# Giving out the last FFN step of each group behind the next group's first score product

## Chip, cores, metric

One core of one Trainium2 chip. The metric is the device time of one execution in microseconds (us), median of several; lower is better. The kernels of an experiment are timed in rounds together with the kernel before, on the same chip. Profiles are taken once per kernel; the profiled span leaves out some 2 us of the time at the ends, so spans are compared with spans and times with times.

## The reference, cut to what matters

```python
# attention: B,H,S,D = 4,8,768,48; a complex gate per element, normalised to a magnitude <= 0.999
for t in range(S):
    S_re, S_im = ar*S_re - ai*S_im + kv, ar*S_im + ai*S_re     # kv = k_t outer v_t
    y[:, :, t] = einsum('bhd,bhde->bhe', q[:, :, t], S_re)
x = y.transpose(0, 2, 1, 3).reshape(3072, 384)
# maxout FFN: d_ff = 768
h = maximum(maximum(x @ w1, x @ w2), x @ w3)
out = h @ w_out
```

## The kernel before

The kernel works in tiles of 128 tokens, two tiles to a group (C = 2), twelve groups. For each tile TensorE makes two score products **A** and **B**, a state product **dk**, transposes **tp** for the next tile, a small product **F**, suffix sums **sfx** and the attention output **y**. Between these the program weaves, as steps in a list, the gates of the next group (activations on ScalarE, products on VectorE and GpSimd, the small matmuls **mds** and **cs**) and the FFN of the group before: nine **up** steps (12 matmuls each for a whole group) and two **out** steps (**op**, 12 matmuls each, one for each tile).

```python
def weave(*streams):                       # steps of each stream spread evenly over its range
    order = []
    for si, (begin, end, steps) in enumerate(streams):
        n = len(steps)
        for i, step in enumerate(steps):
            order.append((begin + (end - begin) * (i + 0.5) / n, si, i, step))
    for _, _, _, step in sorted(order, key=lambda e: e[:3]):
        step()
...
def outputs(x, xs):                        # the y product, then its copy to SBUF, on ScalarE
    ...
    nc.scalar.copy(out=T["xT", xs[-1]][:, :, o:o + P], in_=y)                    # L575
...
def up_step(xs, fp, i):
    ps = psM.tile(...)                                                           # psM: 4 PSUM buffers
    for j in range(2):
        for d in range(KD):
            nc.tensor.matmul(out=ps[:, j], lhsT=ws[i][...], rhs=xT[:, d], ...)   # L589: needs xT
    if i == 0: nc.scalar.copy(out=dst, in_=ps)
    else:      nc.vector.tensor_tensor(out=dst, in0=dst, in1=ps, op=OP.max)      # L594: hT
def out_step(xs, x):
    for f in range(KF):
        nc.tensor.matmul(out=ps, lhsT=hT[:, f, o:o + P], rhs=wo[:, f], ...)      # L600: doesn't need xT
    nc.scalar.copy(out=ot, in_=ps); nc.sync.dma_start(out=out[...], in_=ot)
...
def tile_steps(x):
    return [scores A, gather A, scores B] + tp[:1] + [gather B, state] + tp[1:] + F + ... + [outputs] + ...
...
for g in range(1, NG):
    ...
    ffn = ffn_steps(tokens(g * C - 1))     # nine up, two out (group 1: the FFN of one tile, 9 + 1)
    def feed(n):                           # also called twice from within the gates, before cs
        for _ in range(min(n, len(ffn))):
            ffn.pop(0)()
    weave((0.0, 1.0, tile_steps(g * C) + tile_steps(g * C + 1)), (0.0, 0.7, pre_steps(g + 1, feed)),
          (0.0, 1.0 if g > 1 else 0.5, [call(feed, 1) for _ in ffn]))
for f in ffn_steps(tokens(NX - 1)):        # the tail: the FFN of the last group
    f()
```

The lines of the helpers are the same in the changed kernel, as the change stands below them. Where an experiment adds lines above, its profile shows them two or three higher.

## Time and profile before

| | before |
|---|---|
| time, median of 3 | 742.48 us (742.40 to 744.02) |
| profiled span, mean granted TensorE clock | 740.5 us, 0.970 |
| TensorE busy | 670.2 us, 91% |
| wait of up for xT | 6.6 us in 9 waits |

TensorE is the engine that sets the time; the waits, the steady group and the first groups are shown and read in the prediction below. Two more lines of the page: the shares by engine of the chain of work that ended last, and the costliest group of instructions, whose last field is TensorE's idle time in front of it and what ended most of that.

```profile
PE 71%; issue 13%; DVE 7%; ACT 6%; DMA 1%; POOL 1%; SPq 0%; ACTq 0%; POOLq 0%; DVEq 0%
...
L589 PE MATMUL up<-xT,w 128*128 128x256 f32 (+1 forms) x1404 | 297.5, 365 | 6.7 <-ACT xT L575 6.6
```

ScalarE, 54% busy, still has 6% of the chain: its queue in front of the xT copy.

### The profile page before, as it was taken

Reading aid. Unit: us, or ns where it says so; the run is one execution under the profiler, and the core shown is the slowest. Engines: PE = TensorE matmul, PEld = TensorE weight load, DVE = VectorE, ACT = ScalarE, POOL = GpSimd, SP = SyncE. Lnnn points to the kernel's source line nnn. Section 1 sums busy time; section 2 is a strip of 40 time slices with the busy share of each in tenths; the row PEclk is TensorE's granted clock in tenths of the full one; section 3 lists DMA queues with packets and bytes.
Section 4 is the critical chain, followed back from the end, with each engine's and each line's share of the span. In section 5 each row is a group of like instructions: output and inputs, shape, how many; then the busy total and the mean of one; then the engine's idle time right before and its main releaser. Section 6 shows DMA issues by size and latency. Waiting matters only on the chain.

```text
span 740.5 us, 17637 instructions
## 1 busy us (share of the span) xinstructions
PE 670.2 (91%) x7620; PEld 540.8 (73%) x7620; DVE 521.2 (70%) x718; ACT 400.8 (54%) x677; POOL 117.1 (16%) x121
## 2 busy tenths in 40 slices
PE   1266779789999999999999999999999999999998
PEld 0055668578778878878878778778778778778785
DVE  5999998897857867767757767767767677565210
ACT  6778655567556566466466466466475465322000
POOL 9200000403104004004005005004004004000000
PEclk9687799999999999999999999999999999999999
DMA  9780432140410410410410410410410210000000
GB/s 220 212 187 12 107 108 45 30 91 12 85 35 10 89 34 9 91 34 12 86 34 12 86 34 12 86 34 13 86 34 13 44 34 2 1 23 2 12 12 22
DMA packets 134158, 38.91 MB, mean 53 GB/s; under 512 B 126784, under 2 KB 129856, under 8 KB 134080
## 3 DMA queue, kind: packets, MB, share of 16 engines
q1 hardware_dynamic: 133824, 37.76, 23.0%
q8 instruction: 60, 0.98, 0.6%
q14 instruction: 18, 0.15, 0.1%
q10 hardware_dynamic: 256, 0.01, 0.0%
HBM read 33.03 MB, written 4.72 MB: 51 GB/s over the span
## 4 chain that ended last, share of the span: by engine, by line
PE 71%; issue 13%; DVE 7%; ACT 6%; DMA 1%; POOL 1%; SPq 0%; ACTq 0%; POOLq 0%; DVEq 0%
PE up L589 34%; PE op L600 12%; PE tp L442 5%; PE dk L539 4%; PE B L502 4%; PE y L567 3%; PE A L502 3%; ACT e L106 2%; PE mds L405 2%; PE cs L360 2%; PE sfx L405 2%; PE F L455 2%; ACT L L106 1%; ACT w L106 1%; PE cs L362 1%
## 5 line engine op out<-in xcount | busy, mean ns | idle before, releaser
L589 PE MATMUL up<-xT,w 128*128 128x256 f32 (+1 forms) x1404 | 297.5, 365 | 6.7 <-ACT xT L575 6.6
L589 PEld LDWEIGHTS up<-xT,w 128*128 128x128 f32 x1404 | 247.5, 190 | 46.2 <-ACT xT L575 8.9
L600 PE MATMUL op<-wo,hT 128*128 128x384 f32 x288 | 98.9, 492 | 7.3 <-DVE wo L292 3.9
L338 POOL TENSOR_TENSOR ai<-ai,L 128x768 f32<-128x768 f32 x10 | 25.8, 2578 | 382.4 <-ACT L L106 309.0
L600 PEld LDWEIGHTS op<-wo,hT 128*128 128x128 f32 x288 | 52.9, 191 | 41.5 <-issue 4.3
L594 DVE TENSOR_TENSOR hT<-hT,up 128x512 f32<-128x512 f32 (+1 forms) x78 | 49.8, 640 | 40.2 <-PE up L589 40.1
L469 DVE TENSOR_TENSOR Q<-Q,f 112x512 f32<-112x512 f32 x48 | 41.2, 857 | 42.0 <-ACT f L106 42.0
L444 ACT COPY K<-tp 112x512 f32<-112x512 f32 x48 | 27.9, 582 | 61.1 <-PE tp L442 61.0
L592 ACT COPY hT<-up 128x512 f32<-128x512 f32 (+1 forms) x39 | 21.4, 548 | 69.4 <-PE up L589 69.4
L602 ACT COPY ot<-op 128x384 f32<-128x384 f32 x24 | 11.5, 479 | 86.5 <-PE op L600 86.5
L551 DVE TENSOR_TENSOR g<-g,dk 112x384 f32<-112x384 f32 x40 | 22.1, 552 | 47.9 <-PE dk L539 47.4
L567 PEld LDWEIGHTS y<-atm,vb 128*32 128x32 f32 x1536 | 39.3, 111 | 13.9 <-issue 7.9
L539 PEld LDWEIGHTS dk<-vb,uk 128*112 128x112 f32 x384 | 42.0, 180 | 6.8 <-issue 2.5
L567 PE MATMUL y<-atm,vb 128*32 128x64 f32 x1536 | 46.6, 223 | 0.4 <-DVE atm L520 0.4
L567 PE MATMUL y<-QG,g 112*32 112x64 f32 x1536 | 46.0, 221 | 0.0
L469 DVE TENSOR_TENSOR QB<-Q,f 112x512 f32<-112x512 f32 (+1 forms) x48 | 45.4, 982 | 0.0
L539 PE MATMUL dk<-vb,uk 128*112 128x96 f32 x384 | 42.4, 264 | 3.1 <-issue 2.3
L502 PE MATMUL B<-QB,KB 112*64 112x96 f32 x768 | 37.8, 252 | 7.3 <-DVE QB L469 7.3
L502 PEld LDWEIGHTS B<-QB,KB 112*64 112x64 f32 x768 | 33.8, 140 | 11.5 <-issue 10.9
L405 PE MATMUL mds<-Ln,mid 128*128 128x384 f32 x48 | 23.9, 582 | 20.1 <-POOL cuts L120 15.9
L106 ACT ACTIVATE f<-F 48x296 f32<-48x296 f32 x96 | 39.6, 413 | 1.4 <-PE F L455 0.2
L502 PE MATMUL A<-Q,K 112*64 112x96 f32 x768 | 37.7, 249 | 2.6 <-DVE Q L469 2.4
(111 smaller groups left out, 1111.9 us busy)
## 6 DMA issues: line engine op xcount, KB each, us to landing
ar<-in_a_re_dram SPq DMA_DIRECT2D x24, 192.0 KB, 3.7
ai<-in_a_im_dram SPq DMA_DIRECT2D x24, 192.0 KB, 3.9
k<-in_k_dram SPq DMA_DIRECT2D x24, 192.0 KB, 2.9
q<-in_q_dram SPq DMA_DIRECT2D x24, 192.0 KB, 3.0
vb<-in_v_dram SPq DMA_DIRECT2D x96, 48.0 KB, 2.4
out_dram<-ot SPq DMA_DIRECT2D x24, 192.0 KB, 1.9
raw<-in_moe_w_dram SPq DMA_DIRECT2D x5, 768.0 KB, 6.5
raw<-in_moe_w_out_dram SPq DMA_DIRECT2D x3, 768.0 KB, 4.4
```

The costliest lines, as they stand in the source:

```text
L106: tab(nc.scalar.activation(**kw))
L338: (nc.gpsimd if g > 1 else nc.vector).tensor_tensor(out=ai, in0=ai, in1=L, op=OP.mult)
L405: nc.tensor.matmul(out=ps, lhsT=mat, rhs=T["Ln", g][:, c * DM:(c + 1) * DM], start=True, stop=True)
L442: nc.tensor.transpose(out=tp[0:DD, j], in_=both(T["U" + nm, x], hg * HU + j), identity=ident)
L444: nc.scalar.copy(out=T["K", x][0:DD, hs], in_=tp[0:DD])
L469: nc.vector.tensor_tensor(out=out, in0=in_, in1=f.to_broadcast([DD, H, 2 * n, 8]), op=OP.mult)
L502: nc.tensor.matmul(out=ps[o:o + L64, h // HU, h % HU * 96:h % HU * 96 + 96], lhsT=K[0:DD, h, o:o + L64], rhs=Q[0:DD, 2 * h + c], start=Tru ...
L539: nc.tensor.matmul(out=ps[0:DD, h // HU, h % HU * 96:h % HU * 96 + 96], lhsT=both(T["Uk", x], h), rhs=T["v", x][:, :, h // 2, o:o + D], st ...
L567: nc.tensor.matmul(out=y[32 * (r % 4):32 * (r % 4) + 32, r // 4, c * L64:(c + 1) * L64], lhsT=V[:, c, i, lo:lo + 32] if new else G[0:DD, c ...
L589: nc.tensor.matmul(out=ps[:, j], lhsT=ws[i][:, d, f * P:(f + 1) * P], rhs=xT[:, d], start=(d == 0), stop=(d == KD - 1))
L594: nc.vector.tensor_tensor(out=dst, in0=dst, in1=ps, op=OP.max)
L600: nc.tensor.matmul(out=ps, lhsT=hT[:, f, o:o + P], rhs=wo[:, f], start=(f == 0), stop=(f == KF - 1))
```

## The change

The intent: when the first up step of a group comes up on TensorE, its input xT is not there yet. So the last step of the old list, an out step that needs no xT, is held back and given out first in the next group.

```diff
+    held = []
     for g in range(1, NG):
         load(g + 1, load_v)
         load(g + 2, load_a, load_kq)
-        ffn = ffn_steps(tokens(g * C - 1))
+        ffn = held + ffn_steps(tokens(g * C - 1))
+        held = [ffn.pop()]
         ...
-    for f in ffn_steps(tokens(NX - 1)):
+    for f in held + ffn_steps(tokens(NX - 1)):
         f()
```

## The prediction

> **What bounds the kernel now.** I read the head of the page first, then the list of TensorE's waits, then the timeline of one steady group (C = 2 tiles), engine by engine, and last the two ends of the run, where things differ.

> ```profile
> PE 670.2 (91%) x7620; PEld 540.8 (73%) x7620; DVE 521.2 (70%) x718; ACT 400.8 (54%) x677; POOL 117.1 (16%) x121
> PEclk9687799999999999999999999999999999999999
> ...
> PE cs L360 <- DVE w L356: 13.7, 3, 12.2
> PE up L589 <- ACT xT L575: 6.6, 9, 0.8
> PE op L600 <- DVE hT L594: 3.4, 1, 3.4
> ```

> The three last lines are of TensorE's waits: total, times, longest, in us. TensorE is busy 91% at a full granted clock after the start, and most of its idle time is in the first 160 us; the one wait that comes back is that of the FFN's first up product for xT, nine times. So from the third group on the kernel is as long as its TensorE stream plus 0.8 us per group. The timeline shows what is behind the 0.8 us, TensorE first and ScalarE after it:

> ```profile
> 436.20 1.54 PE L502 MATMUL A<-Q,K 112*64 112x96 f32 x32
> 438.55 2.86 PE L589 MATMUL up<-xT,w 128*128 128x256 f32 x12 [0.81 <-ACT xT L575]
> 441.33 1.54 PE L502 MATMUL B<-QB,KB 112*64 112x96 f32 x32
> ...
> 434.81 0.84 ACT L106 ACTIVATE L<-L 128x768 f32<-128x768 f32 x1
> 435.68 0.85 ACT L106 ACTIVATE w<-L 128x768 f32<-128x768 f32 x1
> 436.43 0.83 ACT L106 ACTIVATE e<-L 128x768 f32<-128x768 f32 x1
> 437.28 0.84 ACT L106 ACTIVATE e<-e 128x768 f32<-128x768 f32 x1
> 438.03 0.46 ACT L575 COPY xT<-y 128x384 f32<-128x384 f32 x1
> ```

> The y product, whose copy xT is, was done when A began at 436.20, but ScalarE has four activations of 0.83 to 0.85 us of the next group's gates queued ahead of the copy. TensorE has only A (1.54 us) to put in between. B, next in its stream, doesn't need xT, but stands behind the up product. The same pattern, 2.35 us from A's start to the up's start, is at the starts of groups 3 to 10 (I looked at 438.55, 493.69 and 548.84 in detail: 2.35 each time), a period of 55.14 us. The start of group 11 has no wait (no gates follow), and the ninth wait, 0.60 us, is in the tail at 705.68.

> [...] xT runs fifth in line although its input was ready some 1.8 us before, and B doesn't pass the waiting up product. [...] the releaser named is the xT copy of data, not a freed buffer. [...] with GpSimd busy, VectorE's KB product takes 2.03 us against 1.22 us. It matters for the rivals, as it makes VectorE late in the middle of a group.

> **The change part by part.** No instruction of work is added or removed. Each group has 11 slots for FFN steps, before filled by 9 up steps and 2 out steps. From group 2 on, the last out step of a group moves into slot 1 of the next group, and the nine up steps move one slot later. The order of the compiled instructions confirms this: A, op, B, tp, up in place of A, up, B, tp; later tp, up, dk in place of tp, op, dk. xT is now wanted only after A, op, B and the transposes (1.47 + 3.97 + 1.48 + 1.02), 7.9 us after A's start, and is there 2.3 us after it (438.49), so the wait should go as a whole.

> The sizes, by starts of one product to the start of the next, as the ends of matmuls are modelled:

> ```profile
> 160.05 1.54 PE L502 MATMUL A<-Q,K 112*64 112x96 f32 x32 [0.68 <-DVE Q L469]
> 161.52 2.86 PE L589 MATMUL up<-xT,w 128*128 128x256 f32 x12
> 164.31 1.54 PE L502 MATMUL B<-QB,KB 112*64 112x96 f32 x32
> ...
> 498.88 2.75 PE L589 MATMUL up<-xT,w 128*128 128x256 f32 x12
> 501.47 1.72 PE L539 MATMUL dk<-vb,uk 128*112 128x96 f32 x16
> ...
> 532.78 4.04 PE L600 MATMUL op<-wo,hT 128*128 128x384 f32 x12
> 536.65 1.72 PE L539 MATMUL dk<-vb,uk 128*112 128x96 f32 x16
> ```

> Group 2 (160.05) has no xT wait: A then costs 1.47 us and the up 2.79 us. With the wait A costs 2.35, up 2.78. So the wait costs 0.88 us. Slot 1 today: 2.35 + 2.78 = 5.13. After: A 1.47, and an op behind a 64-column product 3.97 (the one behind B, 693.54 to 697.51), 5.44 in all: +0.31. Slot 10 today is an op behind a transpose: 3.87. After it is an up behind a transpose: 2.59, -1.28. Per group -0.97 us; the eight groups 3 to 10 give -7.8. In group 11 slot 1 gives +1.18 (no wait to lose) and slot 10 (behind B) 3.97 to 2.79, -1.18: nil.

> **The ends.** The held step has to be paid somewhere. Group 1 now has one out step fewer and the tail one more. In the tail the op (3.97) stands in front of the nine up steps and covers the 0.6 us that they wait for xT: +3.4. In group 1 the lost op is not worth its 3.9 us, because it was partly a filler:

> ```profile
> 138.01 2.75 PE L600 MATMUL op<-wo,hT 128*128 128x384 f32 x8
> 144.17 1.56 PE L600 MATMUL op<-wo,hT 128*128 128x384 f32 x4 [3.41 <-DVE hT L594]
> 146.19 1.53 PE L360 MATMUL cs<-w,upto 128*128 128x384 f32 x4 [0.47 <-DVE w L356]
> ```

> Here VectorE sets the pace: cs waits for w, which ends near 146.05 either way. In the new order A and half of B go ahead of cs, which takes 2.1 us of A and B out of the time behind cs; but from there dk, the transposes, ScalarE's f and VectorE's Q set when group 2's A can start. Worked along that chain with the durations above (VectorE's uk about 0.5 us earlier, ScalarE's K copy held by its table load until 153.77 as now, Q about 0.25 us earlier), A starts near 159.8 in place of 160.05: -0.25. The compiled order puts a third of the held op ahead of this A, where TensorE waits anyway; two thirds run behind it in slot 1 of group 2, 2.7 us, in the place of an up of 2.79: -0.1. Group 2's cs waits 1.07 us for w today, because L318 stood late in VectorE's order and the gates with it (4.59 us of ScalarE idle before 164.51); it is now ahead of Q: -1.1. Slot 10 of group 2: -1.28.

> Sum: -0.25 - 0.1 - 1.1 - 1.28 - 7.8 + 0 + 3.4 = -7.1 us, 742.48 to 735.4. A check by TensorE's idle time: it loses 8 x 0.88 + 1.1 + 0.6 = 8.7 and gains some 2.4 in group 1, in all 6.3, and 0.1 a group of cheaper neighbours: about the same.

> **The rivals.** A, a new wait at cs takes the place of the old one. VectorE is back to back before it:

> ```profile
> 520.48 0.96 DVE L356 TENSOR_TENSOR w<-w,ai 128x768 f32<-128x768 f32 x1
> ...
> 521.80 1.45 PE L360 MATMUL cs<-w,upto 128*128 128x384 f32 x4
> ```

> The slack is 0.36 us. VectorE's order in this stretch changes (one hT maximum now falls between Q and QB, but another leaves from before w), the sum stays the same, and its start, F, stays equally far from cs on TensorE. The first up step behind the y product gets a PSUM buffer that this hT maximum frees, by my reckoning some 0.1 to 0.2 us before it is wanted. If either is late by 0.3 us in every group, 2.4 us are given back: 738. Against: nothing is added between F and cs. B, group 1 and 2 gain nothing, as A is chained to the gates and the removed cs wait stays: 737. C, group 1 is better than I think, as A and B run in its hole: up to 2 us more, 733.5. D, the out copy comes late: ScalarE must now copy ot in the gates' stretch at 441.7, and the transpose copies behind it delay f. It has 1.02 us idle there and 1.73 us later, and lost a copy near the group's end; little. E, one reads the nine waits alone: 742.48 - 6.6 = 735.9, nearly the same by chance, as it leaves out group 2's wait and the loss in group 1.

> **Range and chances.** The steady part is firm, since groups repeat to 0.01 us; group 1 is loose by 1.5 us either way and the small new waits add up to 2.5 us on one side. So I put 735.8, a little over the sum, and 733.5 to 739.0 for 8 in 10. A fall of 2% would need 727.6, 14.9 us less, more than all of TensorE's waits after 130 us together (some 13.5); a rise of 2% would need over 1.3 us lost in each group. Hence 0.01 faster, 0.98 within 2%, 0.01 slower.

> **What would show each step.** Right: no wait of up for xT in groups 3 to 10 or in the tail; a group period of 54.2 us in place of 55.14; A to B with an op in between 5.4 us; an op of 3.97 us in front of 108 up matmuls in the tail; group 2's A near 159.8 and no wait of its cs. Wrong: waits of cs for w, or of the first up behind y for hT, in each group (rival A); a period still over 54.8; group 2's A later than 161 or earlier than 158.

## The result

| | before | after |
|---|---|---|
| time, median | 742.44 us of 4 (742.17 to 744.02) | 738.06 us of 4 (737.74 to 738.50) |
| ratio | | 0.9937 (95%: 0.9920 to 0.9954) |
| profiled span, clock | 740.5 us, 0.970 | 736.0 us, 0.979 |

A ratio is the mean time of one kernel's fast runs over that of the other's fast runs of the same rounds, so it is not quite the ratio of the medians. The change takes off 4.4 us, 0.6%: "same" at 2%, and inside the predicted range, though near its upper end.

Chain and costliest group of the page of the kernel after:

```profile
PE 76%; issue 16%; DVE 3%; ACT 2%; POOL 1%; DMA 1%; SPq 0%; POOLq 0%; ACTq 0%; DVEq 0%
...
L589 PE MATMUL up<-xT,w 128*128 128x256 f32 (+1 forms) x1404 | 296.3, 365 | 0.6 <-ACT xT L575 0.4
```

ScalarE's share of the chain fell from 6% to 2% and up's wait for xT from 6.6 to 0.4 us; that remaining wait is a single one at 68.5 us, before the groups that the change touches. TensorE's waits of the kernel after between 215 and 700 us, that is all of groups 3 to 11, are one line (total, times, longest):

```profile
PE A L502 <- issue: 0.3, 1, 0.3
```

And a steady group, TensorE first, then ScalarE:

```profile
431.41 1.54 PE L502 MATMUL A<-Q,K 112*64 112x96 f32 x32
432.88 4.14 PE L600 MATMUL op<-wo,hT 128*128 128x384 f32 x12
436.95 1.54 PE L502 MATMUL B<-QB,KB 112*64 112x96 f32 x32
...
439.34 2.76 PE L589 MATMUL up<-xT,w 128*128 128x256 f32 x12
...
432.50 0.84 ACT L106 ACTIVATE e<-e 128x768 f32<-128x768 f32 x1
433.25 0.46 ACT L575 COPY xT<-y 128x384 f32<-128x384 f32 x1
```

The xT copy is as late as before, fifth in ScalarE's queue, 1.84 us behind A's start. But now op runs in that time and the first up comes at 439.34, 5.6 us after the copy is done. The next group's A starts at 485.67, so the period is 54.26 us in place of 55.14: 0.88 us less per group. So far the change does what it was made for.

The ends are different. Here TensorE stands idle in front of cs; I call this idle stretch the hole. Group 1, TensorE only:

```profile
140.11 1.04 PE L502 MATMUL B<-QB,KB 112*64 112x96 f32 x18 [1.49 <-DVE QB L469]
145.20 2.90 PE L360 MATMUL cs<-w,upto 128*128 128x384 f32 x4 [4.06 <-DVE w L356]
147.90 1.49 PE L362 MATMUL cs<-w,every 128*128 128x384 f32 x2
```

Without the held op, TensorE has nothing to do for 4.06 us before cs (before, 3.41 us, then four matmuls of op, then 0.47 us). And the four cs matmuls then take 2.70 us from start to start, against 1.37 in the kernel before. The reason stands in the view by windows: the window, its length, busy time and instructions of TensorE, weight loads, VectorE, ScalarE, GpSimd, then the granted clock, DMA share and GB/s. Kernel before:

```profile
145.00:147.00 2.00, 1.53 (x6) 0.68 (x5) 0.96 (x1) 0.48 (x1) 0.00 (x0) 1.00 0.44 86
```

Kernel after:

```profile
145.00:147.00 2.00, 1.80 (x3) 1.18 (x4) 1.12 (x3) 0.14 (x1) 0.00 (x0) 0.50 0.74 141
```

The granted clock is 0.50 behind the hole in the kernel after and 1.00 in the kernel before. The trace has it at 0.50 from 143.94 to 150.77 us, so the work from cs at 145.20 on is done at half speed for 5.6 us.

To compare whole stretches I use the starts of A products as marks, as they are on TensorE's own chain. "A1" is the A of group 1's first tile, "A2" that of group 2's, and so on.

| stretch | before | after | difference | predicted |
|---|---|---|---|---|
| start to A1 (same code) | 112.50 | 111.51 | -0.99 | 0 |
| A1 to A2 | 47.55 | 49.33 | +1.78 | -0.25 |
| A2 to A3 (group 2) | 55.58 | 53.52 | -2.06 | -2.48 |
| A3 to A11 (8 groups) | 441.15 | 434.69 | -6.46 | -7.8 |
| A11 to the end (group 11, tail) | 83.72 | 86.95 | +3.23 | +3.4 |
| span | 740.5 | 736.0 | -4.5 | -7.1 |

The first row is scatter, not the change: over the thirteen profiles, whose code is the same up to there, A1 starts anywhere from 110.15 to 114.00 us. So one span tells little to 2 us, but the stretches behind A1 do. From A2 to the end the two kernels differ by 5.3 us, and this figure repeats: it was 580.45, 580.45 and 580.61 us in three profiles with the old order, and 575.16 and 575.40 us in two of the kernel after.

Two small things in the rows. In group 2 a new wait took 0.48 us, which stands against the 1.07 us of cs that went away:

```profile
176.41 0.91 PE L405 MATMUL mds<-Ln,mid 128*128 128x384 f32 x2 [0.48 <-DVE hT L594]
```

And once in the whole of groups 3 to 10 an A product breaks off and goes on:

```profile
485.67 1.45 PE L502 MATMUL A<-Q,K 112*64 112x96 f32 x29
487.42 0.38 PE L502 MATMUL A<-Q,K 112*64 112x96 f32 x3 [0.30 <-issue]
```

There A takes 2.06 us in place of 1.47, 0.59 more. "issue" means that it waited for nothing the profile shows. The kernel before has such a gap too (at 548.22 us, 0.20 us long), but inside a wait for xT: A to up is 2.35 us there as in the other groups, so it cost nothing. With 8 x 0.88 = 7.04 less and 0.59 more, the row of -6.46 is accounted for. In the tail the held op stands in front of the up steps as expected:

```profile
697.28 4.14 PE L600 MATMUL op<-wo,hT 128*128 128x384 f32 x12
701.25 23.47 PE L589 MATMUL up<-xT,w 128*128 128x256 f32 x108
```

It costs 3.97 us from start to start and covers the old wait.

### The profile page after: what moved, and what is told of

Read it like the earlier page. It is cut to its first block, busy times and chain, and to the rows that moved or that the text cites. A ratio compares the mean times of both kernels' runs of the same rounds, so it can differ in the third digit from the quotient of the medians.

```text
span 736.0 us, 17688 instructions
## 1 busy us (share of the span) xinstructions
PE 671.4 (91%) x7620; PEld 542.0 (74%) x7620; DVE 520.0 (71%) x718; ACT 397.8 (54%) x677; POOL 122.0 (17%) x121
## 4 chain that ended last, share of the span: by engine, by line
PE 76%; issue 16%; DVE 3%; ACT 2%; POOL 1%; DMA 1%; SPq 0%; POOLq 0%; ACTq 0%; DVEq 0%
PE up L589 35%; PE op L600 12%; PE y L567 5%; PE tp L442 4%; PE dk L539 4%; PE A L502 4%; PE B L502 4%; PE mds L405 2%; PE sfx L405 2%; PE F L455 2%; PE cs L360 2%; DMA w<-in_moe_w_dram 1%; PE cs L362 1%; POOL ai L338 1%; DMA carry<-nf 0%
## 5 line engine op out<-in xcount | busy, mean ns | idle before, releaser
L589 PE MATMUL up<-xT,w 128*128 128x256 f32 (+1 forms) x1404 | 296.3, 365 | 0.6 <-ACT xT L575 0.4
L589 PEld LDWEIGHTS up<-xT,w 128*128 128x128 f32 x1404 | 247.5, 190 | 38.6 <-DVE hT L594 1.8
L600 PE MATMUL op<-wo,hT 128*128 128x384 f32 x288 | 100.5, 498 | 3.9 <-DVE wo L292 3.9
L594 DVE TENSOR_TENSOR hT<-hT,up 128x512 f32<-128x512 f32 (+1 forms) x78 | 50.0, 642 | 67.1 <-PE up L589 66.3
L600 PEld LDWEIGHTS op<-wo,hT 128*128 128x128 f32 x288 | 53.0, 190 | 38.2 <-issue 4.4
L469 DVE TENSOR_TENSOR Q<-Q,f 112x512 f32<-112x512 f32 x48 | 41.1, 856 | 42.0 <-ACT f L106 41.8
L469 DVE TENSOR_TENSOR QB<-Q,f 112x512 f32<-112x512 f32 (+1 forms) x48 | 52.7, 1120 | 0.0
L502 PE MATMUL B<-QB,KB 112*64 112x96 f32 x768 | 38.9, 255 | 9.0 <-DVE QB L469 9.0
L502 PEld LDWEIGHTS B<-QB,KB 112*64 112x64 f32 x768 | 34.6, 142 | 16.6 <-issue 13.2
L539 PEld LDWEIGHTS dk<-vb,uk 128*112 128x112 f32 x384 | 42.7, 183 | 4.0 <-issue 2.7
L539 PE MATMUL dk<-vb,uk 128*112 128x96 f32 x384 | 43.1, 267 | 2.3 <-issue 2.3
L364 ACT ACTIVATE t<-cs 128x384 f32<-128x384 f32 x24 | 11.8, 490 | 56.5 <-PE cs L360 46.5
L405 PE MATMUL mds<-Ln,mid 128*128 128x384 f32 x48 | 24.0, 584 | 19.9 <-POOL cuts L120 15.2
L106 ACT ACTIVATE f<-F 48x296 f32<-48x296 f32 x96 | 39.6, 413 | 1.3
L502 PE MATMUL A<-Q,K 112*64 112x96 f32 x768 | 37.6, 249 | 2.1 <-DVE Q L469 1.8
L415 POOL TENSOR_TENSOR q<-E,q 128x384 f32<-128x384 f32 x20 | 39.2, 1962 | 0.0
```

Source lines behind the costliest of these rows:

```text
L106: tab(nc.scalar.activation(**kw))
L405: nc.tensor.matmul(out=ps, lhsT=mat, rhs=T["Ln", g][:, c * DM:(c + 1) * DM], start=True, stop=True)
L415: eng.tensor_tensor(out=hd(T[nm, x]), in0=E, in1=hd(T[nm, x]), op=OP.mult)
L469: nc.vector.tensor_tensor(out=out, in0=in_, in1=f.to_broadcast([DD, H, 2 * n, 8]), op=OP.mult)
L502: nc.tensor.matmul(out=ps[o:o + L64, h // HU, h % HU * 96:h % HU * 96 + 96], lhsT=K[0:DD, h, o:o + L64], rhs=Q[0:DD, 2 * h + c], start=Tru ...
L539: nc.tensor.matmul(out=ps[0:DD, h // HU, h % HU * 96:h % HU * 96 + 96], lhsT=both(T["Uk", x], h), rhs=T["v", x][:, :, h // 2, o:o + D], st ...
```

## The experiments

Open after the result: why A1 to A2 grew by 1.8 us. **Theory "clock"**: the longer hole in TensorE's work lets the granted clock fall, and work at half speed delays all that hangs on cs. **Rival "order"**: the new order (A and part of B ahead of cs, dk and tp behind it) is itself later, and the clock is a side effect. Also asked: was the xT copy really the cause of the steady wait, and is there a better place for the step? Every kernel gave correct results.

### Filling group 1's hole with idle matmuls

Both kernels are the changed one plus matmuls of no use in front of cs; they write the PSUM tile that cs then starts afresh, so the result is not touched. One with 10 that should fill the hole, and one with 6, as a control with the same order of work.

```diff
@@ turns(), in front of the cs product
+            for f in range(10 if g == 2 and c == 0 else 0):      # 6 in the other kernel
+                nc.tensor.matmul(out=ps, lhsT=wo[:, f % KF, 0:P], rhs=wo[:, f % KF], start=True, stop=True)
```

> The changed kernel with 10 idle products (20 matmuls of 128x384, some 6.5 us, results overwritten) put on TensorE ahead of cs in group 1, where it waited 4.06 us for w in the changed kernel and then ran cs at half the granted clock. Theory 1 (the clock fell because TensorE stood idle over 4 us): the hole shrinks to under 2 us, the clock stays at 1.00, the four cs and two further matmuls take 1.37 and 0.7 us in place of 2.70 and 1.41, the A of group 2 starts some 1.8 us earlier, total about 736.3 us although TensorE does 20 matmuls more. Rival (cs is slow from its place in the order, or from VectorE beside it, and the clock follows from nothing done here): cs stays at 2.7 us, total 738 or more.

> The same with 6 idle products (some 3.9 us): the order of all instructions is that of the run with 10, but TensorE then still stands idle some 4.2 us before cs. Theory 1: the clock falls again, cs takes 2.7 us, A and B behind it start slow too, total 738 to 739 us, about 2 us over the run with 10, although 8 matmuls fewer are run. Rival (order of instructions): the same as the run with 10 within 0.5 us.

Ten: 741.08 us (740.86 to 741.70), ratio 0.9974 (0.9954 to 0.9994). Six: 743.65 us (742.84 to 744.88), ratio 1.0007 (0.9987 to 1.0027). The kernel before had 743.71 us on this chip, median of 7. The cs product with 10 and then with 6:

```profile
145.54 1.56 PE L362 MATMUL cs<-w,upto 128*128 128x384 f32 x4 [1.52 <-DVE w L356]
```

```profile
147.60 2.93 PE L362 MATMUL cs<-w,upto 128*128 128x384 f32 x4 [4.09 <-DVE w L356]
```

The two kernels have the same order of instructions but for the matmuls themselves. In group 1 both have A and B behind cs, as the kernel before has. With a hole of 1.52 us cs ran at the full clock, with one of 4.09 us at half, and A1 to A2 took 47.50 us with 10 and 49.15 with 6: the kernel with *less* work on TensorE was 1.65 us slower there. That is for "clock": a fall alone makes such a difference. "Order" it doesn't test, as neither kernel has the new order; an estimate follows under "All profiles together". (The 10 and 6 are source matmuls; the trace counts two for each, 20 and 12.)

The whole time missed what I expected of the 10, though, and the reason was not the clock: the filler changed the compiled order back in another place. A and B were again behind cs, VectorE's product for the next gates stood late again, and the whole held op came in slot 1. Group 2 then took 57.65 us in place of 53.52. So these two kernels show what a fall of the clock costs and are no better versions.

### Holding back from group 2 on

Group 1 keeps its out step, whose last four matmuls lay in the hole before.

```diff
-        held = [ffn.pop()]
+        held = [ffn.pop()] if g > 1 else []
```

> The change from group 2 on only; group 1 keeps its out step. Theory 1: group 1 is as in the kernel before (no hole of 4 us, cs at full clock, A of group 2 near 160.0), group 2 has an out step fewer and ends some 4 us earlier than before, groups 3 to 10 give 0.88 us each, the tail takes back 3.2: about 734.7 us, 3 us under the changed kernel, better than both. Rival (the held step has to be paid in group 2 as TensorE is the bound there in any case, and group 1 gives nothing back): 738 us.

737.61 us (735.64 to 738.33), ratio 0.9920 (0.9899 to 0.9942). The hole was 3.41 us as before, cs at full clock, A1 to A2 47.54 us; the later groups had the same period of 54.26. It missed the 734.7 that I expected, as group 2, with one step fewer, took 53.68 us and not some 4 us less than the changed kernel's 53.52: VectorE is late there, cs waits 1.5 us for w and the next A 0.35 for Q. It looked a little better than the changed kernel (0.9937), so it was run again beside it, below.

### The xT copy on VectorE

If the ScalarE queue is the cause of the steady wait, then moving the copy alone, in the old order, should take the wait away.

```diff
-        nc.scalar.copy(out=T["xT", xs[-1]][:, :, o:o + P], in_=y)
+        if x == xs[-1] and x > C:
+            nc.vector.tensor_copy(out=T["xT", xs[-1]][:, :, o:o + P], in_=y)
+        else:
+            nc.scalar.copy(out=T["xT", xs[-1]][:, :, o:o + P], in_=y)
```

> The kernel before, its step order untouched, but the xT copy of a group's second tile is done by VectorE, which is ahead of the four gate activations. Theory (the 0.88 us a group is ScalarE's queue and nothing else): waits of up for xT in groups 3 to 10 gone, group period 54.2 to 54.3 us in place of 55.14, total about 735.4 us. Rival (the y product's own latency, or VectorE turns late before cs with one instruction more): waits stay or turn into waits of cs for w, total 738 to 742 us.

740.49 us (740.13 to 741.15), ratio 0.9964 (0.9947 to 0.9981). The cause is confirmed: A to up is 1.47 us in all those groups (434.48 to 435.95, for one), no wait. But only about 3 us came of it, not 7 (from A2 to the end, where profiles can be compared to 0.2 us, 578.95 against 580.45: 1.5 us). In the tail the wait stayed, with 0.68 us, now for VectorE's copy. The new line in the list of TensorE's waits, one of its cases, and VectorE just before:

```profile
PE mds L405 <- DVE hT L597: 3.8, 6, 0.7
...
450.27 0.91 PE L405 MATMUL mds<-Ln,mid 128*128 128x384 f32 x2 [0.69 <-DVE hT L597]
...
445.70 0.96 DVE L340 SCALAR_TENSOR_TENSOR w<-w,ai 128x768 f32<-128x768 f32 x1 [1.70 <-POOL ai L338]
```

mds has its operands; what it waits for is a PSUM buffer, which is free when VectorE has taken the maximum of an earlier up product into hT. In VectorE's stream the last maximum ahead of this mds ran at 449.54 (0.68 us), five lines of the timeline behind the product w at 445.70, which waited 1.70 us for GpSimd's ai. With the old order of steps and no wait for xT, TensorE now outruns VectorE here, and most of the 0.88 us comes back as this wait in six groups (0.66 to 0.69 us in five, 0.39 in one): the period is 55.0 us in those (379.48 to 434.48) and 54.3 in one without it (489.50 to 543.79). The changed kernel doesn't have this wait in groups 3 to 10, since its up steps are one slot later and one maximum fewer stands before mds; it has it once, in group 2. So the held step does two things: it covers the copy and it keeps TensorE behind VectorE.

### The changed kernel and "from group 2 on", again

Same edits as before, five rounds, side by side on one chip, to tell 0.9937 from 0.9920.

> The changed kernel unaltered, for comparison on one chip with the three beside it and for how often its clock falls in group 1. Theory (it stands idle for 4.06 us before cs of group 1 and the clock falls): cs there at half clock again, 2.7 us; total 4.5 us under before. If the fall depends on the moment rather than on the length of the hole, cs may be at full clock this time and the A of group 2 some 1.7 us closer to cs (13.9 in place of 15.6 us).

> Held from group 2 on, again, beside the changed kernel on the same chip: some 1.3 us under the changed kernel (0.992 against 0.9937 of before), as it keeps the clock in group 1 (1.7 us) and the out step in the hole there, but has the late gates of group 2 (a cs wait of 1.5 us). Rival: the two are equal within 0.5 us and the first difference was one of chips.

The changed kernel: 738.82 us (737.75 to 740.14), ratio 0.9940 (0.9927 to 0.9953). From group 2 on: 738.49 us (736.51 to 738.75), ratio 0.9930 (0.9917 to 0.9943). The intervals lie over each other; the difference isn't shown. And this time the clock fell in the second kernel too: cs at half speed behind its 3.41 us hole, A1 to A2 48.86 us, with the very code that gave 47.54 before. So behind a hole of 3.41 us the clock falls in some executions and not in others; what tells them apart stands under "All profiles together".

### Spreading group 1's steps

"From group 2 on", with group 1's steps over 0.9 of the group in place of 0.5, to shorten the hole with useful work.

```diff
-              (0.0, 1.0 if g > 1 else 0.5, [call(feed, 1) for _ in ffn]))
+              (0.0, 1.0 if g > 1 else 0.9, [call(feed, 1) for _ in ffn]))
```

> Held from group 2 on, and the ten steps of group 1 spread over 0.9 of the group in place of its first half: A and B come ahead of cs as in the changed kernel, and two up steps and the out step come behind cs, where TensorE waits for VectorE. Theory: gates of group 2 early as in the changed kernel (no cs wait there), less idle in group 1 by some 2 to 3 us; the hole before cs near 3.5 us, so the clock may or may not fall: 734 to 736.5 where before is 742.4, the fastest of all. Rival (group 1 is set by VectorE alone): the same as held from 2 within 0.5 us.

741.18 us (740.01 to 742.25), ratio 0.9972 (0.9959 to 0.9984): wrong. A1 to A2 took 53.45 us, 5.9 more than with 0.5 (4.6 more than in its repetition, whose clock fell too); group 2 gave 1.0 us back, and nothing behind A3 changed. The single hole is gone, but the work in this stretch hangs on VectorE, and TensorE now waits in pieces; the granted clock (column before the last two) fell all the same and stayed down for longer, from 142.42 to 152.66 us:

```profile
142.00:145.00 3.00, 2.22 (x28) 2.22 (x30) 3.00 (x5) 0.80 (x2) 0.00 (x0) 0.57 0.00 0
```

From 138 to 142 us TensorE was busy for 2.04 of 4 us, with no wait over 2.2 us. So it isn't one long hole alone that makes the clock fall. The steps that were moved back then also cost time behind cs; how the 5.9 us divide was not measured.

### Two steps held back

If one step held back covers the wait, do two give more room?

```diff
-        held = [ffn.pop()]
+        held = [ffn.pop(-2), ffn.pop()] if g > 1 else []
```

> As held from group 2 on, but both out steps of a group are held. Theory (the gain is the xT wait and no more, and one step already covers it with over 5 us to spare): group period 54.26 us again, total within 1 us of held from 2. Rival (each step moved back gives something, as steps then start with more of their inputs ready): a shorter period, 53.5 us or less, and 6 us less in all.

745.66 us (744.93 to 746.75), ratio 1.0035 (1.0020 to 1.0049): slower than the kernel before. The period is 54.73 us (488.80 to 543.53), half a us more than with one step, and A11 to the end took 90.79 us, 3.84 more than in the changed kernel: the tail pays a second op. In group 2 one cs waited 3.80 us for w (to 191.54), and the clock fell there too, from 192.16 to 195.57 us. Between 215 and 760 us TensorE's waits have a new first line; under it one case, and the work of VectorE in front of it:

```profile
PE cs L360 <- DVE w L356: 2.2, 8, 0.3
...
521.33 1.53 PE L360 MATMUL cs<-w,upto 128*128 128x384 f32 x4 [0.23 <-DVE w L356]
...
518.65 0.68 DVE L594 TENSOR_TENSOR hT<-hT,up 128x512 f32<-128x512 f32 x1
519.25 0.95 DVE L355 TENSOR_TENSOR w<-w,ar 128x768 f32<-128x768 f32 x1
```

This is the wait that my rival A warned of. From VectorE's Q behind F to w, one hT maximum lies in between in the kernel after; here, with the up steps a slot later still, there are two. The second one puts w back by 0.60 us (518.65 to 519.25), the slack before cs was 0.36, and the wait is 0.23. So one step held back doesn't reach this limit and two do. One group also has a wait of 0.42 us in front of op that the profile puts down to ScalarE; which buffer it was for is open.

### The old and the "from 2" order with the hole filled

Four idle matmuls ahead of group 1's out step, in its own PSUM tile, in the kernel before and in "from group 2 on". They leave the order of all else as it is.

```diff
@@ out_step
+        for f in range(4 if x == 1 else 0):
+            nc.tensor.matmul(out=ps, lhsT=wo[:, f % KF, 0:P], rhs=wo[:, f % KF], start=True, stop=True)
```

> The kernel before with 4 idle products (8 matmuls of 128x384, 2.6 us) in front of the out step of group 1, so that TensorE's hole there shrinks from 3.4 us to under 1 us. Theory (a hole of 3.4 us drops the clock in some executions and not in others: so far not in the profiles of before, of held from 2 the first time and of xT by VectorE, but in those of held from 2 the second time and of two held): cs at full clock, 1.37 us, in every run; the mean 0.5 to 1.2 us under before in spite of 8 matmuls more, and no run of the slow kind. Rival (the idle products push the out step and with it cs): equal to before or slower.

> Held from group 2 on with the same 4 idle products in group 1. Theory: cs of group 1 at full clock in every run, so 0.5 to 1.5 us under held from 2 alone (0.992 and 0.993 of before), that is 0.991 of before, some 736 us where before is 742.4: the fastest of all. Rival: equal to held from 2 or slower.

> The kernel before once more, for its profile alone: whether the clock falls before cs of group 1 after its hole of 3.4 us. Theory: it may (2 of 5 profiles with this hole so far), then cs takes 2.7 us and the distance from cs to the A of group 2 is 15.2 to 15.6 us in place of 13.86. Rival: it never does in this kernel.

The kernel before with filler: 742.35 us (741.60 to 742.63, 6 runs), ratio 0.9985 (0.9973 to 0.9998): 1.1 us under the kernel before in spite of the added matmuls, as expected, though barely clear of the noise. From group 2 on with filler: 737.97 us (736.79 to 739.03), ratio 0.9930 (0.9916 to 0.9943), as without filler, so the expected gain isn't shown in its time. In both profiles the hole is 0.84 us, the clock 1.00 and A1 to A2 47.55 or 47.56. The two against each other, neither with a fall of the clock in its profile, are 4.4 us apart. The kernel before with filler scattered over 1.0 us, the one without over 2.7 us in the ten runs of that chip.

The third of these is the kernel before, unchanged, for one more profile: 741.04 us. This time its cs was slow, without any change of code:

```profile
143.84 2.67 PE L360 MATMUL cs<-w,upto 128*128 128x384 f32 x4
```

So the kernel before, too, loses this time in some of its executions.

### All profiles together

| profile | longest idle before cs, us | cs at | A1 to A2, us | A2 to the end, us | TensorE busy in the emptiest clock window, us |
|---|---|---|---|---|---|
| before | 3.41 | full | 47.55 | 580.45 | 1.56 |
| before again | 3.41 | half | 48.70 | 580.45 | 0.93 |
| before, filled | 0.84 | full | 47.56 | 580.61 | 2.12 |
| after | 4.06 | half | 49.33 | 575.16 | 0.62 |
| after again | 4.05 | half | 48.68 | 575.40 | 0.00 |
| after, 10 idle matmuls | 1.52 | full | 47.50 | 579.68 | 2.26 |
| after, 6 idle matmuls | 4.09 | half | 49.15 | 579.95 | 0.00 |
| from group 2 | 3.41 | full | 47.54 | 575.36 | 1.56 |
| from group 2 again | 3.41 | half | 48.86 | 575.33 | 1.26 |
| from group 2, filled | 0.84 | full | 47.55 | 575.72 | 2.10 |
| two held from group 2 | 3.42 | half | 48.87 | 583.59 | 1.26 |
| xT on VectorE | 3.41 | full | 47.55 | 578.95 | 1.49 |
| group 1 spread | 2.19 | half | 53.45 | 574.24 | 1.54 |

"Full" and "half" are the granted clock. Six profiles at full clock give 47.50 to 47.56 us, six in which it fell 48.68 to 49.33; in the seventh, the spread one, the moved steps add to it. All six at full clock have A and B behind cs. The new order, with A and half of B ahead of cs, was seen with the fallen clock alone. So "order" can only be estimated: in the four old-order profiles with a fall, the loss is half of the time from cs to the end of the half clock (1.15 us for 2.31, 1.32 for 2.65, 1.32 for 2.64 and 1.65 for 3.38). Taken off the changed kernel's two profiles (49.33 us with 5.57 us at half, 48.68 with 3.12), this leaves some 46.5 and 47.1 us at full clock, 0.4 us or more below the kernel before. By this estimate the new order is not later by itself. With one hole of 4.05 us and more it fell in 3 of 3 profiles, with 3.41 or 3.42 in 3 of 6, with 1.52 or less in 0 of 3.

```profile
142.45:145.87 3.42, 1.56 (x4) 0.68 (x4) 3.32 (x6) 0.26 (x2) 0.00 (x0) 1.00 0.00 0
```

In its repetition, the same code, most of the hole lies in one window, and the next window has half the clock:

```profile
139.33:142.74 3.41, 0.93 (x3) 0.66 (x4) 3.31 (x6) 0.90 (x2) 0.22 (x1) 1.00 0.00 0
142.74:146.15 3.41, 3.41 (x6) 1.45 (x6) 1.08 (x2) 0.97 (x2) 0.00 (x0) 0.50 0.58 119
```

I counted this way over the whole of all traces. In the 57 windows at full clock that were followed by half clock TensorE was busy for 1.60 us at most; in the 2475 that were followed by full clock, for 1.49 us at least. So in these runs the fall goes with the work within a window, and with the length of a hole only as far as it empties one; the fillers that put work into the window (10 in one kernel, 4 in the others) kept the clock. The border near 1.5 us is read from these runs alone.

## Why the prediction was right or wrong

The predicted time of 735.8 us was 2.3 below the 738.06 measured; the range and the class held, and the mechanism is the predicted one. By its steps:

- **xT's copy waits in ScalarE's queue, and a held op covers it.** Right. The waits of groups 3 to 10 and of the tail are gone, and with the copy on VectorE those of groups 3 to 10 went without any held step.
- **-0.97 us per group.** Measured -0.88, period 54.26 where 54.2 was said. Slot 10 has the 2.59 us that were predicted (473.25 to 475.84). The term that was off is the op behind A: 4.07 us (432.88 to 436.95), where I took 3.97 from an op behind B. Over eight groups 0.7 us. The trace before had a hint: an up step took 2.79 us behind A (161.52 to 164.31) and 2.70 behind B (198.35 to 201.05). In group 11 I gave the up behind B 2.79 as well; it took 2.69, and there the two slips cancel. The gap of "issue", hidden in a wait before, adds 0.59.
- **Group 2: -2.48.** Measured -2.06. The wait of cs went as predicted. Rival A had a margin of 0.1 to 0.2 us for a PSUM buffer that an hT maximum frees, at the first up behind y. Such a wait did come in this one group, but in front of mds, with 0.48 us.
- **The tail: +3.4.** Measured +3.23.
- **Group 1: "A starts near 159.8 in place of 160.05: -0.25".** This is the step that failed, in sign and size. Measured from A1 it was +1.78 in the profile and +1.13 in its repetition. I asked what hangs on cs, found VectorE to set the pace, and was right in that: cs starts 33.69 us behind A1 in both kernels. What I took as free was taking work out of TensorE's hole there, which grew from 3.41 to 4.06 us: the chain behind cs was summed with durations at full clock. The clock was then at half for cs and what follows, and the four cs matmuls took 2.70 us in place of 1.37. The pair of fillers puts this at 1.65 us with the order of work the same, and repetitions of one code at 1.15 (before) and 1.32 us (from group 2). Whether the new order at full clock would have given the -0.25 was not tried by itself, as the filler in the changed kernel changed the order too; the estimate above, -0.4 or more, speaks for its direction.
- **The sum.** From A2 on I had -6.85 (the sum of -7.1 without the -0.25), and -5.29 was measured: 0.72 for op, 0.59 for the gap, 0.42 in group 2, less 0.17 in the tail. The rest of the way to -4.4 is group 1, net about +0.9. This is less than the 1.1 to 1.8 us that a fall of the clock costs (A1 to A2 48.68 to 49.33 us with it, 47.50 to 47.56 without), as the kernel before has it in some of its runs too; that last step is argued, since only two of its executions were profiled.

The rivals: A put the time at 738, near to what came, for a reason that did not hold: there is no wait of cs for w and none of the first up behind y in groups 3 to 10. It became true when two steps were held back. B is out, as group 2's cs wait went. C, that group 1 would gain, was the opposite of what happened. D is out, no wait on the path names the out copy. E came to its number by leaving out what I listed.

No version clearly beats the changed kernel: holding back from group 2 on, with or without filler, lies at 0.992 to 0.993 against 0.994, with intervals that overlap.

## What to carry to other kernels

A step that is ready whenever it is called is best put where the busiest engine waits for a late input; but ask what it did where it stood, since there it may have covered another hole (here group 1's, 3.41 us with it and 4.06 without), kept a clock up, or kept the engine behind one that frees its buffers (here mds waited up to 0.7 us in six groups of the old order without the wait for xT). When an engine's idle stretch grows, look at the granted clock of the work *after* it (here 0.50 behind a hole of 4.06 us), and at how much the engine works in the stretch around it (here 1.60 us at most in the windows of 3.41 that half clock followed), not only at the length of the wait. Where single profiles scatter by more than the effect, compare stretches between marks on the bounding engine's own chain: here from A2 on the three old-order profiles repeated to 0.2 us while spans differed by 1.6.

## Further measurements

- Windows of 3.41 us with up to 1.60 us of TensorE work were followed by half clock, and of those at full clock none with more. With group 1's steps spread, the clock fell with no wait over 2.2 us.
- Durations differed with the products next to them: twelve op matmuls took 4.07 us between A and B, 3.97 behind B or y and 3.87 behind a transpose, and an up step 2.79 us between A and B and 2.59 behind a transpose. With 0.1 us in each of eight groups this was a sixth of the effect.
- The gap of "issue" came once behind 215 us in the stream of TensorE instructions (twice in one profile), within an A product, at 379.65 us in one profile and between 485 and 600 in the others; it cost 0.59 us in the kernel after.
- The kernel's whole beginning scattered: with the same code, the same product started between 110.15 and 114.00 us.
- A wait that came back group by group had two causes here with the same look: where the xT copy went to VectorE it was a buffer not yet free (mds, 0.7 us at most in six groups); in the kernel before it was late data (up for xT, 0.8 us in groups 3 to 10). The name of the releaser didn't decide it: an hT maximum frees a buffer for mds, but is an operand of op.
